# Order of the DMA issues in an attention stage: later loads, one-hot moves, the first head's operands and the gate's weights

## The chip, the core and the metric

The kernel runs on one core of a Trainium2 chip. The metric is the device time of one execution in microseconds (us). The kernel before took 1594.1 us, the median of three runs (1592.13 to 1594.23).

## What is computed

The reference chains three stages over 1536 tokens (2 batches of 768) with 512 features, all in float32:

- Attention with 8 heads of 64 features per batch, where a query sees only the keys of its own bucket. A bucket is the sign pattern of the vector's product with six random directions (`proj`). Scores are masked, go through a softmax, and weight `v`.
- A mixture of 8 experts (512 to 1024 to 512, ReLU), each applied to all tokens and weighted by a matrix `P`: the exponential of the gate's logits, balanced by 8 alternations of row and column normalization.
- A second mixture of 8 experts in which each token goes to one expert, assigned greedily by descending logit, 192 tokens to an expert.

```
mask = q_bucket[:, :, :, None] == k_bucket[:, :, None, :]
scores = np.where(mask, scale * q @ k.T, -1e9);  attn = softmax(scores);  x = attn @ v
P = balance(exp(x @ w_gate));  x = sum_e P[:, e] * (relu(x @ w1[e]) @ w2[e])
x[assigned == e] -> relu(x @ w1b[e]) @ w2b[e]
```

## The kernel before

The attention stage is a software pipeline written out by hand. The 16 heads are taken as 8 pairs (n = 0 to 7, two heads s = 0 and 1 of one batch), and each pair as 12 tiles of 128 query rows: tiles 0 to 5 of a pair belong to its first head, 6 to 11 to its second (`TU` = 12, r is the tile's number within its pair). Two tiles make a unit. `PLANS` lists, for even and for odd tiles, the steps and how many tiles each lags behind; the loop over t issues them in that order, and with `manual_schedule` every engine, SP included, executes its own instructions strictly in that order.

For a tile, TensorE forms the scores in PSUM from two products (`qk`, L277): `ka`,`qa` carry high and low parts of q and k, `kb`,`qb` another part and, in rows 64 to 127, one-hot rows of the buckets that do the masking. VectorE takes the maximum (L284), ACT the exponential (L289), POOL normalizes `e` (L301), TensorE transposes it (`tr`, L309), ACT and VectorE split it in high and low parts (L317, L321), and TensorE multiplies by V (`av`, L331). The result of a unit leaves through `xa`: for s = 0 ACT writes `xm` and SP moves its lower half to `xc` (L347); for s = 1 ACT writes `x1` (L351; a buffer called x, idle or pz) and SP moves it in two DMAs to `xm` and `xc` (L352, L353). Two tiles later POOL adds them and splits the sum into `X` (`xp`, L363 to L365). `xa` stands in even tiles, eight tiles behind its unit; so the second head's three units leave in r = 2, 4 and 6 of the next pair, and are added in r = 4, 6 and 8.

Beside a pair's tiles its successor is prepared (`prep`, one step in each of r = 0 to 9): r = 0 and 1 transpose q (from `rq`, L170) and split it, r = 2 and 3 do k, r = 4 and 5 compute bucket bits (L199), r = 6 to 9 the one-hots (`hot`, written by ACT, L230). The split operands and one-hots must get to other partitions, and SP's DMAs do that: `stack` collects such moves in `MOVES`, and at the end of a tile SP issues those that were there at its start (L159). So the six q moves come at the end of r = 2, the six k moves at the end of r = 4, two one-hot moves each at the ends of r = 8 and r = 10. Pair 0 is prepared ahead of the loop; its moves are issued at once for the first head, and held back (`HELD`) for the second.

`load(n)` brings a pair's q, k and v from HBM: two DMAs of 192 KB each to `rq`, `rk`, `rv`, which have two buffers each, so pair n + 2 takes the buffers of pair n, and its load waits for their last reader. Loads of pairs 0 and 1 are ahead of the loop; `load(n + 2)` stands in the last tile of pair n:

```
if r in (0, 2) and 0 < n < NP:
    prep_v(n, r // 2 + 2)
if r == TU - 1 and n + 2 < NP:
    load(n + 2)
```

`prep_v` are POOL's splits of `rv` into high and low parts of V (L254, L257). For n > 0 the last two of a pair stand in its tiles 0 and 2; for pair 0 all four stand in the loop's tiles 3, 3, 6 and 8 (`PREP_V`).

Behind the attention stage the first mixture begins: `wgr`, `wgs` are the gate's weights and their split (L465 to L469), `load_w1` and `load_w2` bring and split the first expert's weights (L431, L432, L436, L441), and `rows_to_cols` computes the logits (L480, L481).

Of the kernel before, what the change touches and what calls it, by code (L numbers as in the profile page):

```python
# [9 lines left out]
F32 = mybir.dt.float32  # L10
F32R = mybir.dt.float32r
# [3 lines left out]
AF = mybir.ActivationFunctionType  # L15
OP = mybir.AluOpType
# [22 lines left out]
def rd(x):  # L39
    return x.bitcast(F32)  # L40
# [3 lines left out]
def kernel(ctx, tc, q, k, v, proj, wg1, w1, w2, wg2, w1b, w2b, out):  # L44
    nc = tc.nc
    B, H, S, D = q.shape
    NB = proj.shape[1]
    N, Dm = out.shape
    E = wg1.shape[1]
    F = w1.shape[2]  # L50
    R = S // 128
    NP = B * H // 2
    HP = H // 2
# [4 lines left out]
    consts = ctx.enter_context(tc.tile_pool(name="consts", bufs=1))  # L58
# [10 lines left out]
    ap = actx.enter_context(tc.tile_pool(name="attn", bufs=1))  # L69
# [1 line left out]

    RAW = {}

    def load(n, what="qkv"):
        b, hp = divmod(n, HP)
        for nm, src in (("q", q), ("k", k), ("v", v)):
            if nm in what:
                t = ap.tile([128, R, 2, D], F32, name="r" + nm, bufs=2)
                rows = (slice(0, R // 2), slice(R // 2, R)) if n == 0 and nm != "v" else (slice(0, R),)
                for rs in rows:  # L80
                    for s in range(2):
                        nc.sync.dma_start(t[:, rs, s, :], src[b, 2 * hp + s].rearrange("(p r) d -> p r d", r=R)[:, rs])
                RAW["r" + nm, n] = t

    order = ExitStack()
    order.enter_context(tc.manual_schedule(engines=ENGINES))
    load(0, "qk")
    load(1, "q")
    idle = ap.tile([128, 512], BF, name="idle")
    nc.gpsimd.memset(idle, 0.0)  # L90
    nc.gpsimd.memset(ident, 1.0)
    nc.gpsimd.affine_select(ident, ident, pattern=[[-1, 128]], compare_op=OP.is_equal, fill=0.0,
                            base=0, channel_multiplier=1)
    pj0 = ap.tile([128, NB], F32, name="pj0")
    for s in range(2):
        nc.scalar.dma_start(pj0[64 * s:64 * s + 64], proj)
    nc.gpsimd.memset(zero, 0.0)
    pid = ap.tile([128, NB], I32, name="pid")
    nc.gpsimd.iota(pid, pattern=[[0, NB]], base=0, channel_multiplier=1)
    pj = ap.tile([128, 256], F32, name="pj")  # L100
    nc.gpsimd.memset(pj, 0.0)
    pz = ap.tile([128, 256], F32, name="pz")
    nc.gpsimd.memset(pz, 0.0)
# [15 lines left out]
    def warm(ns):  # L119

        for _ in range(round(ns / 214)):
            nc.tensor.matmul(Op.rearrange("p a b -> p (a b)"), idle[:, :128], idle, start=True, stop=True)

    warm(1500)
    pat = ap.tile([128, 2, 128], F32R, name="pat")
    pjh = ap.tile([128, 256], F32R, name="pjh")
    pjl = ap.tile([128, 256], F32R, name="pjl")
# [14 lines left out]

    HELD = []

    def stack(n, s, moves):

        if n == 0 and s == 1 and HELD is not None:
            HELD.append((n, s, moves))
            return
        MOVES.extend((dst[at:at + 64, s], src[64 * s:64 * s + 64]) for dst, at, src in moves)  # L150
        if n == 0:
            move()

    MOVES = []

    def move(n=None):

        for dst, src in MOVES[:n]:
            nc.sync.dma_start(rd(dst), rd(src))  # L159
        del MOVES[:n]  # L160

    def prep_t(n, nm, ch, part):
        x = RAW["r" + nm, n]
        c0, c1 = PC[ch]
        if part == 0:
            if ch == 0:
                PREP[nm, n] = [ap.tile([128, S], F32R, name=nm + x, bufs=2 if nm == "q" else 1) for x in ("hi", "lo")]
            t = aps.tile([128, 512], F32, name="tp", bufs=3)
            for r in range(c0 // 128, c1 // 128):
                nc.tensor.transpose(t[:, r * 128 - c0:r * 128 - c0 + 128],  # L170
                                    x[:, r].rearrange("p h d -> p (h d)"), ident)
            PREP["t"] = t[:, :c1 - c0]
            return
        hi, lo = PREP[nm, n]
        t = PREP["t"]
        if part == 1:
            nc.scalar.activation(hi[:, c0:c1], t, AF.Copy, scale=scale if nm == "q" else 1.0)
            return
        if nm == "q":
            nc.vector.scalar_tensor_tensor(lo[:, c0:c1], t, scale, rd(hi[:, c0:c1]), op0=OP.mult, op1=OP.subtract)  # L180
        else:
            nc.vector.tensor_tensor(lo[:, c0:c1], t, rd(hi[:, c0:c1]), op=OP.subtract)
        if ch == 0:
            return
        qa, ka, qb, kb = ST[n % 2]
        for s in range(2):
            stack(n, s, ((qa, 0, hi), (qa, 64, hi), (qb, 0, lo)) if nm == "q" else ((ka, 0, hi), (ka, 64, lo), (kb, 0, hi)))

    def prep_bits(n, ch, part):
        c0, c1 = PC[ch]  # L190
# [16 lines left out]
    def hot_rows(dst, t, w, s, on_dve=False):  # L207

        rows = slice(64 * s, 64 * s + 64)
        if on_dve:  # L210
            nc.vector.tensor_scalar(dst, t[rows], 0.5 * NB if w else 0.5 * (NB - 2), 1.0 if w else BIG,
                                    op0=OP.is_ge if w else OP.is_gt, op1=OP.subtract if w else OP.mult)
        else:
            nc.scalar.activation(dst, t[rows], AF.Sign if w else AF.Relu, bias=cb[rows, w:w + 1], scale=1.0 if w else BIG)

    def prep_hot(n, w, ch, part):
        c0, c1 = PC[ch]
        if part == 0:
            if ch == 0 and n:
                PREP["o", w, n] = ap.tile([128, S], F32R, name=f"hot{w}", bufs=1)  # L220
            t = (Sp[1] if n == 0 and w == ch == 1 else aps.tile([128, 512], F32, name="tp", bufs=3))[:, :c1 - c0]
            nc.tensor.matmul(t, pat[:, w], PREP["b", n][:, c0:c1], start=True, stop=True)
            PREP["t"] = t
        if part == 1 and n == 0:
            for s in range(2):
                hots0[s].append((ST[0][2 + w][64:128, s, c0:c1], PREP["t"], w, s))
            hot_rows(*hots0[0].pop(), on_dve=w != ch)
        elif part == 1:
            hot = PREP["o", w, n]
            nc.scalar.activation(hot[:, c0:c1], PREP["t"], AF.Sign if w else AF.Relu, bias=cb[:, w:w + 1],  # L230
                                 scale=1.0 if w else BIG)
            if ch == 1:
                dst = ST[n % 2][2 + w]
                for s in range(2):
                    stack(n, s, ((dst, 64, hot),))

    def prep(n, i, part):
        if i < 4:
            prep_t(n, "qk"[i // 2], i % 2, part)
        elif i < 6:  # L240
            prep_bits(n, i - 4, part)
        else:
            prep_hot(n, (i - 6) // 2, i % 2, part)
# [18 lines left out]
    TU = 4 * U  # L262
# [109 lines left out]
    def ahead_v(t):  # L372
        n, r = divmod(t, TU)
        for i in range(4):
            if t == PREP_V[i]:
                prep_v(0, i)
        if r in (8, 10) and n + 1 < NP:
            prep_v(n + 1, r // 2 - 4)
        if r in (0, 2) and 0 < n < NP:
            prep_v(n, r // 2 + 2)  # L380
        if r == TU - 1 and n + 2 < NP:
            load(n + 2)

    STEPS = dict(qk=qk, soft=soft, expo=expo, inv=inv, norm=norm, tr=tr, th=trh, tl=trl, av=av, xa=xa, xp=xp, pp=lambda t: ahead(t, 0), pa=lambda t: ahead(t, 1), pd=lambda t: ahead(t, 2),
# [28 lines left out]
    core = ctx.enter_context(tc.tile_pool(name="core", bufs=1, reuse_waits="tile"))  # L413
# [4 lines left out]
    def small_ps():  # L418
        return ps.tile([128, 512], F32, name="sp", bufs=2)
# [45 lines left out]
    wgr = core.tile([128, HP, E], F32, name="wgr")  # L465
    nc.sync.dma_start(wgr, wg1.rearrange("(a p) e -> p a e", p=128))
    wgs = core.tile([128, HP, 2 * E], F32R, name="wgs")
    nc.vector.tensor_copy(wgs[:, :, :E], wgr)
    nc.vector.tensor_tensor(wgs[:, :, E:], wgr, rd(wgs[:, :, :E]), op=OP.subtract)  # L469
# [27 lines left out]
    t = small_ps()  # L497
# [276 lines left out]
    for blk in range(NX):  # L774
        Hs.append((as_h(bigx() if blk else big()), as_h(big())))
        if blk == NX - 1:
# [5 lines left out]
            hot = hotp[:, :C * HC // 2].bitcast(F16).rearrange("p (c n) -> p c n", c=C)  # L782
# [434 lines left out]
```

## Time and profile before

| | us |
|---|---|
| Median of three runs | 1594.1 |
| The profiled execution, its own time | 1593.44 |
| Span of that execution, first to last instruction | 1591.7 |
| TensorE (PE) busy | 1548.0 |
| VectorE (DVE) busy | 809.2 |
| ACT busy | 453.2 |
| POOL busy | 269.9 |

The attention stage ends at about 270 us of the span; the first mixture fills the time to about 1279 us and the second the rest. A row of a timeline gives the start, the length, the engine and line, what is written from what, and how many instructions were merged; in brackets stands how long the engine stood idle before it and what it is thought to have waited for. SPq and ACTq are DMA issues on the queues of SP and ACT: their length is that of the issue, not of the transfer. L numbers are lines of the kernel before.

### The profile page before, as it was taken

To read this page: it belongs to the slowest core of one execution; us is meant where nothing else is said; L and a number is where in the kernel's file an instruction comes from. 1 tells how busy PE (TensorE), PEld (TensorE's weight loads), DVE (VectorE), ACT (ScalarE), POOL (GpSimd) and SP (SyncE) were. 2 spreads that over 40 slices of the span, in tenths; PEclk is the share of its full clock that TensorE was granted. 3 is DMA by queue.
4 is the path that set the end of the run, shared out by engine and by line. 5 is a ranking of instruction groups with operands and counts; after the bars stand their busy time and mean duration, and the time that the engine had idled before them with its cause. 6 is when DMAs were issued, how large, how long until landed. Compare 5 with 4: busy or idle time off the path is not lost.

```text
span 1591.7 us, 21428 instructions
## 1 busy us (share of the span) xinstructions
PE 1548.0 (97%) x8482; PEld 1311.2 (82%) x8482; DVE 809.2 (51%) x1833; ACT 453.2 (28%) x855; POOL 269.9 (17%) x313
## 2 busy tenths in 40 slices
PE   7999998999999999999999999999999999999998
PEld 6888886788888888888888888888887767788998
DVE  6888886712433334333333332134676377567533
ACT  6787886211211211221221021021121210011343
POOL 4888887020000000000000000000000000111221
PEclk9999999999999999999999999999999999899999
DMA  8766662220200110120020020011000116545531
GB/s 190 167 146 164 147 138 66 67 93 0 93 14 14 66 40 1 53 67 1 27 93 1 14 80 27 0 54 53 1 14 14 40 40 224 180 180 183 195 136 31
DMA packets 89301, 123.84 MB, mean 78 GB/s; under 512 B 44336, under 2 KB 52016, under 8 KB 89200
## 3 DMA queue, kind: packets, MB, share of 16 engines
q1 hardware_dynamic: 81680, 109.88, 23.7%
q0 software_dynamic: 2176, 6.29, 1.3%
q10 hardware_dynamic: 5344, 6.30, 1.1%
q8 instruction: 67, 1.10, 0.3%
q14 instruction: 34, 0.28, 0.1%
HBM read 83.91 MB, written 9.44 MB: 59 GB/s over the span
## 4 chain that ended last, share of the span: by engine, by line
PE 85%; DMA 4%; ACT 3%; DVE 2%; SPq 2%; POOL 2%; issue 1%; POOLq 0%; ACTq 0%; DVEq 0%
PE hp L567 32%; PE yp L586 29%; PE hp L944 5%; PE yp L888 4%; PE yp L997 3%; PE S L277 2%; PE O L331 2%; PE tp L309 2%; PE yp L1000 1%; PE sp L1081 1%; ACT e L289 1%; DMA rq<-in_q_dram 1%; SPq L159 1%; PE tp L199 1%; DMA raw<-in_moe_w_dram 1%
## 5 line engine op out<-in xcount | busy, mean ns | idle before, releaser
L567 PE MATMUL hp<-X,big 128*128 128x512 f32 x2304 | 528.9, 390 | 0.0
L567 PEld LDWEIGHTS hp<-X,big 128*128 128x128 f32 x2304 | 431.7, 188 | 89.9
L586 PE MATMUL yp<-big 128*128 128x512 f32 x2016 | 461.2, 389 | 0.0
L586 PEld LDWEIGHTS yp<-big 128*128 128x128 f32 x2016 | 378.2, 188 | 78.4
L568 ACT ACTIVATE big<-hp 128x512 fp32r<-128x512 f32 x176 | 105.2, 598 | 755.9 <-PE hp L567 755.9
L569 DVE SCALAR_TENSOR_TENSOR big<-hp,big 128x512 fp32r<-128x512 f32 x176 | 121.6, 691 | 252.3 <-ACT big L568 252.3
L591 DVE SCALAR_TENSOR_TENSOR acc<-yp,P,acc 128x512 f32<-128x512 f32 x72 | 54.1, 751 | 258.4 <-PE yp L586 258.4
L869 POOL DMA_INDIRECT raw<-x2h,who x4 | 4.1, 1025 | 949.5 <-DVE wg2b L1066 939.1
L301 POOL TENSOR_TENSOR e<-e,w 128x768 f32<-128x768 f32 x96 | 138.9, 1468 | 42.7 <-DVE w L296 27.5
L321 DVE TENSOR_TENSOR al<-tp,ah 128x512 fp32r<-128x512 f32 x144 | 98.2, 683 | 15.8 <-ACT ah L317 13.3
L284 DVE TENSOR_REDUCE w<-S 128x1 f32<-128x768 f32 x96 | 91.3, 951 | 14.8 <-PE S L277 13.4
L944 PE MATMUL hp<-raw,big 128*128 128x192 f32 x488 | 93.7, 338 | 1.2 <-ACT raw L922 1.2
L317 ACT ACTIVATE ah<-tp 128x512 fp32r<-128x512 f32 x144 | 86.2, 600 | 25.2 <-PE tp L309 22.2
L289 ACT ACTIVATE e<-S,w 128x768 f32<-128x768 f32 x96 | 87.0, 906 | 2.0 <-DVE w L284 1.9
L309 PE MATMUL tp<-ident,e 128*128 128x128 f32 x576 | 84.6, 274 | 2.2 <-POOL e L301 2.1
L432 DVE TENSOR_TENSOR big<-raw,big 128x1024 fp32r<-128x1024 f32 x63 | 76.6, 1222 | 14.1 <-ACT big L431 14.0
L944 PEld LDWEIGHTS hp<-raw,big 128*128 128x128 f32 x488 | 79.7, 193 | 2.8 <-ACT raw L922 1.7
L431 ACT ACTIVATE big<-raw 128x1024 fp32r<-128x1024 f32 x63 | 64.9, 1054 | 34.1 <-DMA raw<-in_moe_w_dram 32.8
L331 PE MATMUL O<-ah,vv 128*128 128x256 f32 x288 | 72.9, 283 | 1.3 <-ACT xm L346 0.8
L331 PE MATMUL O<-al,vv 128*128 128x256 f32 x288 | 72.9, 282 | 0.0
L309 PEld LDWEIGHTS tp<-ident,e 128*128 128x128 f32 x576 | 66.5, 141 | 4.8 <-POOL e L301 3.7
L542 DVE SCALAR_TENSOR_TENSOR junk<-acc,wg2b 128x512 bf16<-128x512 f32 x96 | 66.0, 687 | 1.9
(257 smaller groups left out, 1578.3 us busy)
## 6 DMA issues: line engine op xcount, KB each, us to landing
raw<-in_moe_w_dram SPq DMA_DIRECT2D x67, 512.0 KB, 3.4
big<-in_moe_w_dram SPq DMA_DIRECT2D x32, 1024.0 KB, 7.5
qa<-qhi SPq DMA_DIRECT2D x32, 192.0 KB, 3.8
qb<-qlo SPq DMA_DIRECT2D x16, 192.0 KB, 4.1
ka<-khi SPq DMA_DIRECT2D x16, 192.0 KB, 4.3
ka<-klo SPq DMA_DIRECT2D x16, 192.0 KB, 4.0
kb<-khi SPq DMA_DIRECT2D x16, 192.0 KB, 4.3
rv<-in_v_dram SPq DMA_DIRECT2D x16, 192.0 KB, 4.3
```

The lines of the kernel that those rows point to most:

```text
L284: nc.vector.tensor_reduce(EN[t][:, 0, i:i + 1], Sp[i], op=OP.max, axis=AX.X, negate=True)
L289: nc.scalar.activation(e, Sp[i], AF.Exp, bias=w[:, 0, i:i + 1], scale=1.0, accum_out=w[:, 1, i:i + 1])
L301: nc.gpsimd.tensor_tensor(e, e, w[:, 3, i:i + 1].to_broadcast([128, S]), op=OP.mult)
L309: nc.tensor.transpose(p[:, y * 128:y * 128 + 128], EN[t + i][:, kt * 128:kt * 128 + 128], ident)
L317: nc.scalar.activation(ah, TP[t, x], AF.Copy)
L321: nc.vector.tensor_tensor(al, TP[t, x], rd(ah), op=OP.subtract)
L331: nc.tensor.matmul(o, VS[n][:, kt, s].rearrange("p a d -> p (a d)"), a[:, :, kt], start=(kt == 0 and a is ah), stop=(kt == R - 1 and a is al))
L567: nc.tensor.matmul(t, a, b, start=(i == 0), stop=(i == len(prods) - 1))
L568: nc.scalar.activation(hh[:, f], t, AF.Relu)
L569: nc.vector.scalar_tensor_tensor(hl[:, f], t, 0.0, rd(hh[:, f]), op0=OP.max, op1=OP.subtract)
L586: nc.tensor.matmul(t, a, b, start=(i == 0), stop=(i == len(prods) - 1))
L944: nc.tensor.matmul(opened[f], w[:, d, f * 128:f * 128 + 128], xt[:, d], start=(d == 0), stop=(d == HP - 1))
```

## The change

- `load` gets a `queue` argument. At the start q of pair 0 is loaded on SP, then the projection (`pj0`) in one DMA and k of pair 0 on ACT's queue; six idle products warm TensorE and not seven.
- `pj` shares its buffer with an `x1` buffer.
- For the first head of pair 0 the operand rows are copied by engines: the three of q by POOL, two of k by ACT; only `klo` into `ka` goes by DMA.
- The one-hots of later pairs are moved at once, right behind ACT's writing of the second half, and not through `MOVES`.
- `load(n + 2)` stands in r = 3 and not in r = 11.
- The gate's weights are loaded ahead of the loop and split in tile 12, and not behind the attention stage.

```
--- before.py
+++ after.py
@@ -71,7 +71,7 @@
 
     RAW = {}
 
-    def load(n, what="qkv"):
+    def load(n, what="qkv", queue=None):
         b, hp = divmod(n, HP)
         for nm, src in (("q", q), ("k", k), ("v", v)):
             if nm in what:
@@ -79,25 +79,26 @@
                 rows = (slice(0, R // 2), slice(R // 2, R)) if n == 0 and nm != "v" else (slice(0, R),)
                 for rs in rows:
                     for s in range(2):
-                        nc.sync.dma_start(t[:, rs, s, :], src[b, 2 * hp + s].rearrange("(p r) d -> p r d", r=R)[:, rs])
+                        (queue or nc.sync).dma_start(t[:, rs, s, :],
+                                                     src[b, 2 * hp + s].rearrange("(p r) d -> p r d", r=R)[:, rs])
                 RAW["r" + nm, n] = t
 
     order = ExitStack()
     order.enter_context(tc.manual_schedule(engines=ENGINES))
-    load(0, "qk")
+    load(0, "q")
+    pj0 = ap.tile([128, NB], F32, name="pj0")
+    nc.scalar.dma_start(pj0, bass.AP(tensor=proj.tensor, offset=proj.offset, ap=[[0, 2], [NB, D], [1, NB]]))
+    load(0, "k", nc.scalar)
     load(1, "q")
     idle = ap.tile([128, 512], BF, name="idle")
     nc.gpsimd.memset(idle, 0.0)
     nc.gpsimd.memset(ident, 1.0)
     nc.gpsimd.affine_select(ident, ident, pattern=[[-1, 128]], compare_op=OP.is_equal, fill=0.0,
                             base=0, channel_multiplier=1)
-    pj0 = ap.tile([128, NB], F32, name="pj0")
-    for s in range(2):
-        nc.scalar.dma_start(pj0[64 * s:64 * s + 64], proj)
     nc.gpsimd.memset(zero, 0.0)
     pid = ap.tile([128, NB], I32, name="pid")
     nc.gpsimd.iota(pid, pattern=[[0, NB]], base=0, channel_multiplier=1)
-    pj = ap.tile([128, 256], F32, name="pj")
+    pj = ap.tile([128, 256], F32, name="x1")
     nc.gpsimd.memset(pj, 0.0)
     pz = ap.tile([128, 256], F32, name="pz")
     nc.gpsimd.memset(pz, 0.0)
@@ -121,7 +122,7 @@
         for _ in range(round(ns / 214)):
             nc.tensor.matmul(Op.rearrange("p a b -> p (a b)"), idle[:, :128], idle, start=True, stop=True)
 
-    warm(1500)
+    warm(1300)
     pat = ap.tile([128, 2, 128], F32R, name="pat")
     pjh = ap.tile([128, 256], F32R, name="pjh")
     pjl = ap.tile([128, 256], F32R, name="pjl")
@@ -142,14 +143,21 @@
 
     HELD = []
 
-    def stack(n, s, moves):
+    def stack(n, s, moves, nm=None):
 
         if n == 0 and s == 1 and HELD is not None:
             HELD.append((n, s, moves))
             return
-        MOVES.extend((dst[at:at + 64, s], src[64 * s:64 * s + 64]) for dst, at, src in moves)
-        if n == 0:
-            move()
+        for dst, at, src in moves:
+            to, x = dst[at:at + 64, s], src[64 * s:64 * s + 64]
+            if n:
+                MOVES.append((to, x))
+            elif s or (nm, at) == ("k", 64):
+                nc.sync.dma_start(rd(to), rd(x))
+            elif nm == "q":
+                nc.gpsimd.tensor_copy(to, rd(x))
+            else:
+                nc.scalar.activation(to, rd(x), AF.Copy)
 
     MOVES = []
 
@@ -184,7 +192,7 @@
             return
         qa, ka, qb, kb = ST[n % 2]
         for s in range(2):
-            stack(n, s, ((qa, 0, hi), (qa, 64, hi), (qb, 0, lo)) if nm == "q" else ((ka, 0, hi), (ka, 64, lo), (kb, 0, hi)))
+            stack(n, s, ((qa, 0, hi), (qa, 64, hi), (qb, 0, lo)) if nm == "q" else ((ka, 0, hi), (ka, 64, lo), (kb, 0, hi)), nm)
 
     def prep_bits(n, ch, part):
         c0, c1 = PC[ch]
@@ -232,7 +240,7 @@
             if ch == 1:
                 dst = ST[n % 2][2 + w]
                 for s in range(2):
-                    stack(n, s, ((dst, 64, hot),))
+                    nc.sync.dma_start(rd(dst[64:128, s]), rd(hot[64 * s:64 * s + 64]))
 
     def prep(n, i, part):
         if i < 4:
@@ -378,7 +386,7 @@
             prep_v(n + 1, r // 2 - 4)
         if r in (0, 2) and 0 < n < NP:
             prep_v(n, r // 2 + 2)
-        if r == TU - 1 and n + 2 < NP:
+        if r == 3 and n + 2 < NP:
             load(n + 2)
 
     STEPS = dict(qk=qk, soft=soft, expo=expo, inv=inv, norm=norm, tr=tr, th=trh, tl=trl, av=av, xa=xa, xp=xp, pp=lambda t: ahead(t, 0), pa=lambda t: ahead(t, 1), pd=lambda t: ahead(t, 2),
@@ -397,7 +405,13 @@
         stack(*x)
     load(0, "v")
     load(1, "v")
+    wgr = consts.tile([128, HP, E], F32, name="wgr")
+    nc.sync.dma_start(wgr, wg1.rearrange("(a p) e -> p a e", p=128))
+    wgs = consts.tile([128, HP, 2 * E], F32R, name="wgs")
     for t in range(NT + max(x[1] for x in PLANS[0])):
+        if t == TU:
+            nc.vector.tensor_copy(wgs[:, :, :E], wgr)
+            nc.vector.tensor_tensor(wgs[:, :, E:], wgr, rd(wgs[:, :, :E]), op=OP.subtract)
         due = len(MOVES)
         for nm, lag, *part in PLANS[t % 2]:
             if 0 <= t - lag < NT:
@@ -462,11 +476,6 @@
     ones = core.tile([128, 128], F32, name="ones")
     nc.gpsimd.memset(ones, 1.0)
 
-    wgr = core.tile([128, HP, E], F32, name="wgr")
-    nc.sync.dma_start(wgr, wg1.rearrange("(a p) e -> p a e", p=128))
-    wgs = core.tile([128, HP, 2 * E], F32R, name="wgs")
-    nc.vector.tensor_copy(wgs[:, :, :E], wgr)
-    nc.vector.tensor_tensor(wgs[:, :, E:], wgr, rd(wgs[:, :, :E]), op=OP.subtract)
     acc = core.tile([128, C, Dm], F32, name="acc")
 
     def rows_to_cols(stat, movs, dst):
```

## Rows read from the trace of the kernel before

**Rows 1.** The page: busy time of TensorE, and the exponential's group (busy us, mean ns).

```profile
PE 1548.0 (97%) x8482; PEld 1311.2 (82%) x8482; DVE 809.2 (51%) x1833; ACT 453.2 (28%) x855; POOL 269.9 (17%) x313
...
L289 ACT ACTIVATE e<-S,w 128x768 f32<-128x768 f32 x96 | 87.0, 906 | 2.0 <-DVE w L284 1.9
```

**Rows 2.** Busy time by stages: sum of six pair spans, 42.74 to 233.10 us.

```profile
sum 190.36, PE 178.02 PEld 167.20 DVE 163.85 ACT 155.85 POOL 160.84; mean PE 29.67 PEld 27.87 DVE 27.31 ACT 25.97 POOL 26.81
```

**Rows 3.** TensorE's waits, 0 to 275 us: us in total, times, longest.

```profile
PE S L277 <- DMA kb<-hot: 5.3, 6, 1.2
PE tp L170 <- DMA rq<-in_q_dram: 4.8, 4, 1.7
PE sp L480 <- DVE wgs L469: 4.3, 1, 4.3
...
PE tp L170 <- DVE w L296: 1.7, 2, 0.9
```

**Rows 4.** Timeline of SP's queue in pair 2: start, us of issue, line, transfer.

```profile
88.02 0.88 SPq L352 DMA_DIRECT2D xm<-idle  x1
88.95 0.85 SPq L353 DMA_DIRECT2D xc<-idle  x1
...
95.14 0.95 SPq L353 DMA_DIRECT2D xc<-pz  x1
...
104.11 1.34 SPq L82 DMA_DIRECT2D rq<-in_q_dram  x2
...
106.93 1.78 SPq L82 DMA_DIRECT2D rv<-in_v_dram  x2
```

**Rows 5.** Timeline of POOL in pair 2 (in brackets its wait, and for what).

```profile
88.00 2.89 POOL L301 TENSOR_TENSOR e<-e,w 128x768 f32<-128x768 f32 x2
91.72 0.74 POOL L363 TENSOR_TENSOR xm<-xm,xc 128x256 f32<-128x256 f32 x1 [0.82 <-DMA xc<-idle]
...
93.23 0.74 POOL L365 TENSOR_TENSOR X<-xm,X 128x256 fp32r<-128x256 f32 x1
...
98.01 0.73 POOL L363 TENSOR_TENSOR xm<-xm,xc 128x256 f32<-128x256 f32 x1
...
100.19 2.90 POOL L301 TENSOR_TENSOR e<-e,w 128x768 f32<-128x768 f32 x2
```

**Rows 6.** Timeline of TensorE in pair 2: transposes of `e`.

```profile
96.80 0.60 PE L309 MATMUL tp<-ident,e 128*128 128x128 f32 x4
...
101.72 0.66 PE L309 MATMUL tp<-ident,e 128*128 128x128 f32 x4
```

**Rows 7.** Line L82, all loads: time from issue to landing.

```profile
DMA to landing us min/median/max: 2.4/3.9/4.7
```

**Rows 8.** Timeline of SP's queue, the start and the end of pair 0.

```profile
2.92 2.08 SPq L82 DMA_DIRECT2D rk<-in_k_dram  x4
...
9.36 1.45 SPq L159 DMA_DIRECT2D ka<-klo  x1
...
17.56 0.91 SPq L159 DMA_DIRECT2D kb<-khi  x1
...
39.22 0.46 SPq L347 DMA_DIRECT2D xc<-xm  x1
39.72 1.24 SPq L159 DMA_DIRECT2D kb<-hot  x2
```

**Rows 9.** Timeline of TensorE: first score product of pair 0, second of pair 1.

```profile
13.65 0.62 PE L277 MATMUL S<-ka,qa 128*128 128x512 f32 x2 [2.15 <-DMA ka<-klo]
...
42.74 0.59 PE L277 MATMUL S<-kb,qb 128*128 128x512 f32 x2 [1.17 <-DMA kb<-hot]
```

**Rows 10.** Timeline of POOL: the last V copy of pair 0 (tile 8).

```profile
38.88 1.02 POOL L257 TENSOR_TENSOR vv<-rv,vv 128x384 fp32r<-128x384 f32 x1
```

**Rows 11.** By stages behind attention: us, busy by engine, granted clock, DMA share, GB/s.

```profile
269.50:273.80 4.30, 0.01 (x2) 0.01 (x1) 0.44 (x2) 0.38 (x1) 3.37 (x6) 1.00 0.45 94
274.00:278.00 4.00, 4.00 (x12) 1.36 (x11) 1.06 (x1) 1.83 (x2) 1.09 (x3) 0.57 0.92 334
```

More of the change, by code (lines that the diff above doesn't have):

```diff
@@ L72, with load @@
     RAW = {}
-    def load(n, what="qkv"):
+    def load(n, what="qkv", queue=None):
         b, hp = divmod(n, HP)
@@ L81, in load @@
                     for s in range(2):
-                        nc.sync.dma_start(t[:, rs, s, :], src[b, 2 * hp + s].rearrange("(p r) d -> p r d", r=R)[:, rs])
+                        (queue or nc.sync).dma_start(t[:, rs, s, :],
+                                                     src[b, 2 * hp + s].rearrange("(p r) d -> p r d", r=R)[:, rs])
                 RAW["r" + nm, n] = t
@@ L86 @@
     order.enter_context(tc.manual_schedule(engines=ENGINES))
-    load(0, "qk")
+    load(0, "q")
+    pj0 = ap.tile([128, NB], F32, name="pj0")
+    nc.scalar.dma_start(pj0, bass.AP(tensor=proj.tensor, offset=proj.offset, ap=[[0, 2], [NB, D], [1, NB]]))
+    load(0, "k", nc.scalar)
     load(1, "q")
@@ L93 @@
                             base=0, channel_multiplier=1)
-    pj0 = ap.tile([128, NB], F32, name="pj0")
-    for s in range(2):
-        nc.scalar.dma_start(pj0[64 * s:64 * s + 64], proj)
     nc.gpsimd.memset(zero, 0.0)
@@ L99 @@
     nc.gpsimd.iota(pid, pattern=[[0, NB]], base=0, channel_multiplier=1)
-    pj = ap.tile([128, 256], F32, name="pj")
+    pj = ap.tile([128, 256], F32, name="x1")
     nc.gpsimd.memset(pj, 0.0)
@@ L122, in warm @@
             nc.tensor.matmul(Op.rearrange("p a b -> p (a b)"), idle[:, :128], idle, start=True, stop=True)
-    warm(1500)
+    warm(1300)
     pat = ap.tile([128, 2, 128], F32R, name="pat")
@@ L143, with stack @@
     HELD = []
-    def stack(n, s, moves):
+    def stack(n, s, moves, nm=None):
         if n == 0 and s == 1 and HELD is not None:
@@ L149, in stack @@
             return
-        MOVES.extend((dst[at:at + 64, s], src[64 * s:64 * s + 64]) for dst, at, src in moves)
-        if n == 0:
-            move()
+        for dst, at, src in moves:
+            to, x = dst[at:at + 64, s], src[64 * s:64 * s + 64]
+            if n:
+                MOVES.append((to, x))
+            elif s or (nm, at) == ("k", 64):
+                nc.sync.dma_start(rd(to), rd(x))
+            elif nm == "q":
+                nc.gpsimd.tensor_copy(to, rd(x))
+            else:
+                nc.scalar.activation(to, rd(x), AF.Copy)
     MOVES = []
@@ L186, in prep_t @@
         for s in range(2):
-            stack(n, s, ((qa, 0, hi), (qa, 64, hi), (qb, 0, lo)) if nm == "q" else ((ka, 0, hi), (ka, 64, lo), (kb, 0, hi)))
+            stack(n, s, ((qa, 0, hi), (qa, 64, hi), (qb, 0, lo)) if nm == "q" else ((ka, 0, hi), (ka, 64, lo), (kb, 0, hi)), nm)
     def prep_bits(n, ch, part):
@@ L234, in prep_hot @@
                 for s in range(2):
-                    stack(n, s, ((dst, 64, hot),))
+                    nc.sync.dma_start(rd(dst[64:128, s]), rd(hot[64 * s:64 * s + 64]))
     def prep(n, i, part):
@@ L380, in ahead_v @@
             prep_v(n, r // 2 + 2)
-        if r == TU - 1 and n + 2 < NP:
+        if r == 3 and n + 2 < NP:
             load(n + 2)
@@ L399 @@
     load(1, "v")
+    wgr = consts.tile([128, HP, E], F32, name="wgr")
+    nc.sync.dma_start(wgr, wg1.rearrange("(a p) e -> p a e", p=128))
+    wgs = consts.tile([128, HP, 2 * E], F32R, name="wgs")
     for t in range(NT + max(x[1] for x in PLANS[0])):
+        if t == TU:
+            nc.vector.tensor_copy(wgs[:, :, :E], wgr)
+            nc.vector.tensor_tensor(wgs[:, :, E:], wgr, rd(wgs[:, :, :E]), op=OP.subtract)
         due = len(MOVES)
@@ L463 @@
     nc.gpsimd.memset(ones, 1.0)
[L465 to L469, printed above, removed]
     acc = core.tile([128, C, Dm], F32, name="acc")
```

## The prediction

> **What bounds the kernel now.** I read the page's busy times first: TensorE is busy for 1548.0 of 1591.7 us [rows 1], so only the stretches where it waits can give time back. The rest of the kernel behind the attention stage (two expert stages) is touched by the change only in its first microseconds, and I carry it over unchanged. The view by stages then shows the attention stage: six spans from one pair's start to the next take 190.36 us together, 31.73 each, with TensorE busy for 178.0 and POOL for 160.8 of them [rows 2]. TensorE idles 2.06 us a pair and POOL 4.9, so POOL is a second resource that is nearly full. Third, the list of TensorE's waits up to 275 us [rows 3] says where its idle time lies: 5.3 us on `kb<-hot` (six pair starts), 4.8 on `rq` (four pair starts), 1.7 more at the same place, the first transposes of `rq`, put down to a VectorE instruction long done, so I count it to `rq` too, and 4.3 us once on the gate's weights. Per pair start that is 0.88 for the one-hots and (4.8 + 1.7)/6 = 1.08 for `rq`, 1.96 together. The change attacks these.
>
> Last I read SP's own order within one pair, and POOL's and TensorE's beside it. This is where I expect the result to be decided. From its second tile on SP issues without a break: x moves, six q moves, x moves (88.02 and 88.95, the latter ending 89.80), six k moves, x moves (the last ends 96.09) [rows 4]. POOL needs each of these x moves two tiles later: it was free at 90.89 (88.00 + 2.89) and stood until 91.72 for `xc` (0.82 us); the next, at 98.01, came just in time [rows 5]. Behind the x additions POOL normalizes the next two tiles, from 100.19 on; the first is done at 101.64, and TensorE transposes it at 101.72 [rows 6]. So at this point the chain SP, POOL, TensorE has no slack at all.
>
> **The change part by part.**
>
> *Loads in the fourth tile.* They were issued in a pair's last tile, after the one-hots: 104.11 to 108.71, six issues, 4.6 us [rows 4]. They now stand in SP's order behind the six q moves and ahead of the x moves of tile 4. What they give: `rq` is there long before it is transposed, 1.08 us a pair start. What they cost: everything behind them on SP comes later by six issues. In the start of the program four such issues took 2.08 us, so six take 3.1 at least [rows 8]; 4.6 is the row of the same six; I take 4.4, nearest to the latter, because the transfers around them are as dense. Then `xc` of tile 4 lands at 96.1 and not at 91.72; POOL, free at 90.89, idles 5.2 us in place of 0.82. Its three additions (91.72 to 93.97, 2.25 us) and two normalizations (2.90) end at 101.25, one V copy (1.02 at most [rows 10]) by 102.3. The k moves and x moves behind the load end 4.4 later too: the last x move at 100.5, landing 1.92 later (89.80 to 91.72) at 102.4. So POOL's next x addition starts at 102.4 in place of 98.01, the normalization at 104.65 in place of 100.19, and TensorE's transpose moves from 101.72 to 106.1, 4.4 later; the one before it (96.80) moves by some 3.0. At the pair's end the two waits of 1.96 are gone. Net +2.4 us a pair. POOL works off its own delay in its other idle time, so the next pair starts from TensorE's delay alone and the amount repeats. It applies to pairs 1 to 5: pair 0 has no x additions, pairs 6 and 7 load nothing. 5 x 2.44 = **+12.2**. Bounds: 3.1 - 1.96 = 1.2 a pair (+5.8 in all); 4.6 and another 1.1 because the x moves' data may queue behind the load's (a load lands 3.9 after its issue [rows 7], the x move 91.72 - 88.95 = 2.8) less 1.96 = 3.7 a pair (+18.7).
>
> *The same load in pair 0.* `rv` has two buffers, and `rv` of pair 2 takes that of pair 0. Its last reader is the V copy that stands in tile 8, while the load now stands in tile 3. SP therefore stops at `rv` until POOL has done tile 8's copy (38.88 + 1.02 = 39.90 [rows 10]). Behind it on SP wait pair 1's k moves, all its one-hots and the x moves. With the faster start below (4.0 us) the release is at 35.9. Then two `rv` issues (1.8) to 37.7, six k moves (89.80 to 95.14 less one x issue of 0.9, 4.4) to 42.1, two one-hots of q (1.2) to 43.3, one x issue (0.5) to 43.8, and the first one-hot of k, which takes 3.0 from issue to use (39.72 to 42.74 [rows 8, 9]): 46.8 against 42.74, +4.1. Less the 0.9 of `rq` (half of 1.7 [rows 3]): +3.2. TensorE comes to this product at 42.74 - 1.17 - 4.0 = 37.6 [rows 9], so it has stood for 9.2 us. After 4.3 us of standing at 269.5 the granted clock was 0.57 for the next 4.0 us [rows 11], a loss of 1.7. Pair 1 so starts **+4.9** later than before (bounds +2.2, with a start faster by 5 and no loss of clock, to +6.4, with a start faster by 2.5).
>
> *The start itself.* Four `rk` issues go from SP (from 2.92) to ACT's queue behind one issue of `pj0`, so from about 1.4; bounded by nothing (if the transfers are what is slow) and 2.08, I take 1.3 on the last `k` residual. The `klo` move was issued at 9.36 behind three others and the first score product waited for it until 13.65, 4.3 us [rows 8, 9]; alone it should take 3.0, as the one-hot's did, so the product starts 2.5 earlier. Five moves less on SP and the transfers also bring the second head's `kb<-khi` (issued at 17.56, and waited for by pair 1's first k split) forward by about 5. Three POOL copies of 768 elements, about 1.45 each by the normalization's row (two of 768 elements in 2.90 [rows 5]), stand where POOL has nothing to do; two ACT copies at about 0.9 (the exponential's 768 elements, 906 ns [rows 1]) lie between the k splits and the one-hots, where ACT waited for TensorE. I take 4.0 for the start (2.5 to 5). All of it is contained in the +4.9 above: the release of SP hangs on it, and what was gained ahead of it is stood out at pair 1's start.
>
> *One-hots at once.* Now issued right after ACT wrote them, a tile and a half earlier, ahead of the x move that SP waited at. Six of the seven pair starts are settled above; the last gives **-0.9**. If SP stood at them for ACT, only an x move would be behind, needed four tiles later.
>
> *Gate's weights early.* TensorE's 4.3 us [rows 3] are mostly not on the path: the first expert's weights, split by ACT and VectorE, come later. What is on it is one SP issue ahead of these loads (0.6) and a shorter gate among VectorE's splits. I take **-1.2** (-0.6 to -2.5). The two small VectorE operations in tile 12 cost nothing while SP's moves hold TensorE there, 0.4 us at most otherwise. One idle warm-up product less lies beside `rq`'s arrival: 0.
>
> **Sum.** 12.2 + 4.9 - 0.9 - 1.2 = +15.0 against the profiled execution's 1593.4 us (span 1591.7; the median shown, 1594.1, is 0.04% above it): **1608 us**. The lowest sum of the bounds is 5.8 + 2.2 - 0.9 - 2.5 = +4.6 (1598), the highest 18.7 + 6.4 - 0.9 - 0.6 = +23.6 (1617).
>
> **The clock in each pair.** The row shows a clock of 0.57 after 4.3 us without work [rows 11]; a wait of 3 us in the middle of pairs 1 to 5 is not in this trace, and the sum above keeps 1.00 there. The Trainium skill ("TensorE: Matmul & The Clock Gate", HAM oscillation) has it that a wait that comes back in every pass of a loop can throw the array to its lower clock in every pass. By that rule the sum would be 1616.9, by the rows alone 1608.4; the trace agrees with it for the one long wait at 269.5 and shows nothing for shorter ones.
>
> **The rivals.**
> 1. *Faster: POOL absorbs the late x moves.* Place: the x addition of tile 6. If `xc` came no later than POOL is ready, by less than about 1.96 us net at TensorE, the pair starts' gain is kept. For it: POOL idles 4.9 us a pair. Against it: POOL already waits here, and 101.64 to 101.72 leaves 0.1. With none of the delay at TensorE: -9.8 in place of +12.2, 1586.4.
> 2. *SP isn't held in pair 0*, so pair 1 starts earlier by 4.0 + 1.17 + 0.9 = 6.1, and not later by 4.9: 1597.4; with rival 1 as well 1575.5. Against it: the reader of tile 8 is in the code.
> 3. *The clock falls in each pair:* 1.7 each, 8.5: 1616.9.
> 4. *The delay and the gain cancel* (a delay of 2 us a pair and a short hold in pair 0): about 1594.
>
> **How the numbers follow.** Forecast (1598 to 1617) 0.58; rival 3 0.08; rival 2 alone 0.10; rival 1, with or without 2, 0.17; rival 4 0.07. A difference under 0.2% (3.2 us) can't be told from none here. Slower: 0.58 + 0.08 and most of rival 2, 0.75; same: rival 4 and an edge, 0.07; faster: 0.18. The range that leaves out rival 1's half and the far end of rival 3 is 1589 to 1618.
>
> **What would show it.** In the new trace: SP's `rq`, `rk`, `rv` issues between q moves and x moves; POOL's wait for `xc<-idle` at some 5 us in pairs 1 to 5 (0.8 now); TensorE waiting for POOL's `e` by 3 to 4 us in the ninth tile; pair spans of about 34 us in place of 31.7; no wait for `rq`; SP standing 10 us before the third `rv`, and TensorE 8 us at pair 1's start. Wrong it would be if pair spans are under 31.5, or if pair 1 starts before 42.7.

## The result, and the profile after

The changed kernel takes **1612.52 us** (median of 4 runs, 1611.03 to 1618.63); the kernel before, on the same chip, 1593.12 (1591.51 to 1594.23). The ratio is 1.013, 95% interval 1.0102 to 1.0158: 19.4 us slower. The forecast was 1608 (1589 to 1618). The profiled execution of the changed kernel is its longest, 1618.63 us (span 1616.8), so its trace overstates the loss by about 6 us. In `prep`, `soft` and `tr` every line stands 8 further down than before (the normalization L301 is now L309, the transposes L309 are L317).

The page again begins with the busy times, beside [rows 1]:

```profile
PE 1562.4 (97%) x8481; PEld 1326.7 (82%) x8481; DVE 808.2 (50%) x1833; ACT 453.4 (28%) x857; POOL 271.8 (17%) x316
```

TensorE has one instruction less and 14.4 us more busy time. Most of that is work at a lower clock. The five passes from pair 1's first `rq` transpose to pair 6's show it by stages. The columns are the stretch and its us, then the busy time of each engine, granted clock, DMA share, GB/s. First the kernel before, then the changed one:

```profile
45.35:76.85 31.50, 29.65 (x221) 27.89 (x221) 27.14 (x49) 26.10 (x56) 26.95 (x25) 1.00 0.70 157
...
sum 158.97, PE 148.60 PEld 139.36 DVE 136.83 ACT 130.62 POOL 134.80; mean PE 29.72 PEld 27.87 DVE 27.37 ACT 26.12 POOL 26.96
```

```profile
49.92:87.23 37.31, 32.68 (x221) 31.16 (x221) 26.34 (x46) 25.51 (x55) 25.77 (x24) 0.86 0.57 133
...
sum 180.05, PE 158.54 PEld 150.35 DVE 134.09 ACT 129.51 POOL 133.65; mean PE 31.71 PEld 30.07 DVE 26.82 ACT 25.90 POOL 26.73
```

The passes went from 31.8 to 36.0 us each, 21.1 in all: 9.9 of it is longer TensorE work on the same instructions, 11.1 idle time. The first row's start also says that pair 1 begins 4.6 later. What is left of attention behind them, 0.6 shorter, and the gate, another 0.6 shorter, give little back.

Where TensorE waits, up to 295 us (us in total, times, longest), beside [rows 3]:

```profile
PE tp L317 <- POOL e L309: 23.3, 8, 4.6
PE S L285 <- DMA kb<-hot: 5.5, 1, 5.5
...
PE tp L178 <- DMA rq<-in_q_dram: 0.4, 1, 0.4
```

The waits that the change attacked are gone: `rq` has 0.4 us left, `kb<-hot` is left once, in pair 1, and the gate's weights are not in the list. In their place TensorE waits for POOL's normalized tiles, 23.3 us, once in each of pairs 1 to 5 by 4.0 to 4.6. POOL's own wait is this one:

```profile
POOL xm L371 <- DMA xc<-idle: 32.8, 5, 7.0
```

SP's queue in pair 2 says why, beside [rows 4]:

```profile
97.97 2.07 SPq L82 DMA_DIRECT2D rq<-in_q_dram  x2
100.09 1.34 SPq L82 DMA_DIRECT2D rk<-in_k_dram  x2
101.53 1.45 SPq L82 DMA_DIRECT2D rv<-in_v_dram  x2
103.08 0.84 SPq L360 DMA_DIRECT2D xm<-idle  x1
103.97 0.59 SPq L361 DMA_DIRECT2D xc<-idle  x1
```

The six loads hold SP from 97.97 to 102.98, 5.0 us, and the x moves stand behind them. POOL (beside [rows 5]) is free at 101.36, waits 6.2 us, and everything that it does after that is late. TensorE (beside [rows 6]) stands at 111.29:

```profile
98.47 2.89 POOL L309 TENSOR_TENSOR e<-e,w 128x768 f32<-128x768 f32 x2
107.59 0.73 POOL L371 TENSOR_TENSOR xm<-xm,xc 128x256 f32<-128x256 f32 x1 [6.23 <-DMA xc<-idle]
```

```profile
111.29 1.11 PE L317 MATMUL tp<-ident,e 128*128 128x128 f32 x4 [4.02 <-POOL e L309]
```

### The profile page after: what moved, and what is told of

Read it like the earlier page. It is cut to its first block, busy times and chain, and to the rows that moved or that the text cites. A ratio compares the mean times of both kernels' runs of the same rounds, so it can differ in the third digit from the quotient of the medians.

```text
span 1616.8 us, 21450 instructions
## 1 busy us (share of the span) xinstructions
PE 1562.4 (97%) x8481; PEld 1326.7 (82%) x8481; DVE 808.2 (50%) x1833; ACT 453.4 (28%) x857; POOL 271.8 (17%) x316
## 3 DMA queue, kind: packets, MB, share of 16 engines
q8 instruction: 66, 1.08, 0.3%
## 4 chain that ended last, share of the span: by engine, by line
PE 89%; DMA 3%; DVE 3%; POOL 2%; ACT 2%; issue 1%; SPq 0%; ACTq 0%; POOLq 0%; DVEq 0%
PE hp L576 32%; PE yp L595 28%; PE hp L953 5%; PE yp L897 4%; PE O L339 3%; PE tp L317 3%; PE S L285 3%; PE yp L1006 3%; PE yp L1009 1%; PE sp L1090 1%; DMA xc<-idle 1%; PE tp L207 1%; POOL e L309 1%; PE yp L1011 1%; PE tp L178 1%
## 5 line engine op out<-in xcount | busy, mean ns | idle before, releaser
L309 POOL TENSOR_TENSOR e<-e,w 128x768 f32<-128x768 f32 x96 | 138.9, 1468 | 35.3 <-DVE w L304 25.7
L317 PE MATMUL tp<-ident,e 128*128 128x128 f32 x576 | 89.5, 285 | 23.3 <-POOL e L309 23.3
L317 PEld LDWEIGHTS tp<-ident,e 128*128 128x128 f32 x576 | 70.3, 147 | 26.0 <-POOL e L309 24.9
L339 PE MATMUL O<-ah,vv 128*128 128x256 f32 x288 | 76.4, 293 | 1.4 <-ACT xm L354 0.9
L445 ACT ACTIVATE big<-raw 128x1024 fp32r<-128x1024 f32 x63 | 64.7, 1053 | 33.8 <-DMA raw<-in_moe_w_dram 32.5
```

Of the source, the lines that this page charges most:

```text
L309: nc.gpsimd.tensor_tensor(e, e, w[:, 3, i:i + 1].to_broadcast([128, S]), op=OP.mult)
L317: nc.tensor.transpose(p[:, y * 128:y * 128 + 128], EN[t + i][:, kt * 128:kt * 128 + 128], ident)
L339: nc.tensor.matmul(o, VS[n][:, kt, s].rearrange("p a d -> p (a d)"), a[:, :, kt], start=(kt == 0 and a is ah), stop=(kt == R - 1 and a is al))
```

## The experiments

Each edit is to the changed kernel unless it says otherwise; `r` is the tile within a pair, `TU` its 12 tiles. Each ratio is to the kernel before on the same chip. The runs stand on several chips, on which the kernel before took 1593.1 to 1594.5 us, so some differences are given by the ratios too.

**Load back in the last tile** (the rest of the change stays):

```diff
-        if r == 3 and n + 2 < NP:
+        if r == TU - 1 and n + 2 < NP:
```

> The changed kernel with the loads of later pairs back in a pair's last tile; all else of the change stays. Theory A (the load's place in SP's queue is what costs: x moves behind it reach POOL late in pairs 1 to 5, and SP is held in pair 0): POOL's wait for xc falls from 6 to 7 us a pair to under 1, pair spans from about 35.4 to 30 to 30.7 us, pair 1 starts near 37 us, and the time is 1576 to 1584 us, clearly under the kernel before. Theory B (the cost lies in another part: engine copies, one-hots at once, or the early gate): the time stays above 1600 us and pair spans above 33.

1578.76 us (1574.64 to 1580.11), ratio 0.9909 (0.9889 to 0.993). So the move of the loads costs 33.8 us (1612.52 - 1578.76), and all else in the change gains 14.4. The waits of TensorE, of POOL, and the five passes:

```profile
PE tp L178 <- DMA rq<-in_q_dram: 2.5, 4, 0.9
...
PE tp L178 <- DVE w L304: 1.5, 1, 1.5
```

```profile
POOL xm L371 <- DMA xc<-idle: 2.4, 5, 0.8
```

```profile
sum 152.07, PE 147.23 PEld 139.22 DVE 139.46 ACT 130.22 POOL 134.27; mean PE 147.23 PEld 139.22 DVE 139.46 ACT 130.22 POOL 134.27
```

POOL's wait is back at under 1 us a pair, and the passes are 30.4 us, against 31.8 before the change. The expectation of 1576 to 1584 us held. At the first transposes of `rq` TensorE still waits: 4.7 us in six pair starts by the timeline, against 6.5 before. So there an earlier load had up to 4.7 us left to give.

**The two halves of the move.** Only pair 0's load back in the last tile, and its opposite, only pair 0's load in the fourth:

```diff
+        if r == (3 if n else TU - 1) and n + 2 < NP:     # first kernel
+        if r == (TU - 1 if n else 3) and n + 2 < NP:     # second kernel
```

> The changed kernel with pair 0's load alone back in its last tile; pairs 1 to 5 load in their fourth. Theory A: SP is not held before the third rv, pair 1 starts 8 to 9 us earlier than the 47.0 of the changed kernel and without the slow clock behind it, 1600 to 1604 us; pair spans of pairs 1 to 5 stay at 35 to 36. Rival (the hold in pair 0 only takes up time that would be lost anyway): under 3 us gained, 1609 to 1613.

> The changed kernel with the early load in pair 0 alone; pairs 1 to 5 load in their last tile. Theory A: the hold stays (pair 1 starts near 47), pair spans fall from 35.4 to 30 to 30.7: 1585 to 1592 us. Rival (pair 0's hold is most of the loss): above 1600. If the two places add up, this run's gain and that of the run with pair 0 last sum to the gain of the run with all loads last.

The first takes 1605.62 us (1603.06 to 1607.28; ratio 1.0076, 1.0059 to 1.0093): without pair 0's hold 6.9 are back, and the kernel is still slower than before (1600 to 1604 was expected). The second takes 1584.21 (1582.34 to 1589.01; ratio 0.9943, 0.9926 to 0.9959): the hold alone costs 5.4 against the loads in the last tile (1585 to 1592 was expected). The effects add up within 1.4 us: undoing the move in pair 0 gains 6.9, undoing it in the other pairs 28.3 (1612.52 - 1584.21), 35.2 together, against 33.8 in one. POOL's wait in the first and TensorE's in the second:

```profile
POOL xm L371 <- DMA xc<-idle: 33.7, 5, 7.1
```

```profile
PE S L285 <- DMA kb<-hot: 5.6, 1, 5.6
```

**The load's move alone, and the one-hots alone**, each put into the kernel before:

```diff
-        if r == TU - 1 and n + 2 < NP:      # first kernel
+        if r == 3 and n + 2 < NP:
-                    stack(n, s, ((dst, 64, hot),))      # second kernel
+                    nc.sync.dma_start(rd(dst[64:128, s]), rd(hot[64 * s:64 * s + 64]))
```

> The kernel before with one part of the change alone, the loads in the fourth tile. Theory A: without the faster start SP is released at 39.9 us, pair 1 starts near 51 us, pair spans go to 35 to 36: 1616 to 1628 us, slower than the changed kernel. Rival (the load's place is harmless by itself and the loss comes with another part): 1580 to 1593 us, as the waits for rq go.

> The kernel before with the one-hots moved at once, nothing else. Theory: 0.88 us at each of seven pair starts go, and the loads, now issued 1.2 us earlier behind one move less, give part of the 1.08 for q: 1581 to 1588 us. Rival (the next wait at the pair start takes its place): 1591 to 1594 us.

The loads alone: 1626.73 us (1625.65 to 1627.27), ratio 1.0212 (1.0195 to 1.0229). That is 33.5 over the 1593.21 beside it, the same price as in the changed kernel (33.8). TensorE's waits show both faults at once, POOL's late tiles and the one-hots in the list of moves: one wait of 6.1 at pair 1's start, behind pair 0's hold, and five of about 1.1, as before the change:

```profile
PE tp L309 <- POOL e L301: 25.2, 7, 5.8
...
PE S L277 <- DMA kb<-hot: 11.4, 6, 6.1
```

The one-hots alone: 1584.56 us (1583.4 to 1588.39), ratio 0.9941 (0.9921 to 0.9962), 9.9 us faster than the 1594.47 beside it. Its five passes:

```profile
sum 151.90, PE 147.41 PEld 139.35 DVE 137.09 ACT 129.47 POOL 133.71; mean PE 147.41 PEld 139.35 DVE 137.09 ACT 129.47 POOL 133.71
```

That is the same 30.4 a pass as with the rest of the change and late loads. One line, with the loads where they were, brings TensorE's idle time in the passes from 10.4 us (158.97 - 148.60) to 4.5. Nearly all of what is left stands at the first transposes of `rq`, 4.5 us in six pair starts by the timeline (6.5 before): that is what an earlier load could still have given.

**Does the clock cost?** Behind each of these five waits the granted clock is at or near 0.50 for some 4 to 6 us; that is the lower of its two levels (1.2 of 2.4 GHz). In the next kernel TensorE transposes the identity while it would stand, in pairs 1 to 5:

```diff
+        if x == 0 and t % TU == 4 and 1 <= t // TU <= 5:
+            for _ in range(32):
+                nc.tensor.transpose(p[:, :128], ident, ident)
```

> The changed kernel with 32 idle transposes on TensorE ahead of the first transposes of tile 8 in pairs 1 to 5, where it stands 4.0 to 4.6 us waiting for POOL (about 3.5 us of work that nobody reads). Theory: the lower clock behind that wait costs 1.7 us a pair; with TensorE kept at work the granted clock stays at 1.00 there, POOL's waits stay as they are, pair spans fall from 36.0 by 1.5 to 2, and the time is 1602 to 1606 us. Rival (POOL sets the pace, the clock costs nothing): 1611 to 1614, or more by the work added.

1611.85 us (1611.51 to 1613.53), ratio 1.0104 (1.0086 to 1.0122): 0.7 less than 1612.52, or 4 by the ratios (1.013 and 1.0104), whose intervals overlap, so the two are not told apart. The five passes take 177.35 us, 2.7 less than the 180.05 of the changed kernel; the expectation was 1.5 to 2 for each. A stretch with the clock, in the changed kernel (TensorE stood for 4.63 us until 76.08) and with the filling (columns as above); then TensorE's and POOL's rows with the filling:

```profile
74.00:80.00 6.00, 3.92 (x16) 3.73 (x17) 1.65 (x2) 1.95 (x4) 5.84 (x7) 0.50 0.55 139
```

```profile
74.00:80.00 6.00, 4.52 (x35) 4.14 (x34) 2.46 (x4) 3.57 (x7) 5.84 (x8) 1.00 0.50 129
```

```profile
75.66 0.66 PE L320 MATMUL tp<-ident,e 128*128 128x128 f32 x4 [1.48 <-POOL e L309]
81.50 0.66 PE L320 MATMUL tp<-ident,e 128*128 128x128 f32 x4 [1.11 <-POOL e L309]
```

```profile
71.96 0.73 POOL L374 TENSOR_TENSOR xm<-xm,xc 128x256 f32<-128x256 f32 x1 [7.29 <-DMA xc<-idle]
```

The clock is at its higher level, and TensorE then waits for POOL at the next tile. POOL is busy for 5.84 of the 6 us in both: it sets the pace here, and most of the time of the slow matmuls lay beside it.

**Issues or bytes?** For pairs 2 to 7 the six loads stay in their places, but each brings 8 KB into a scratch tile, and the pair is computed from the data of pairs 0 and 1 (so the output is another; pair 0's hold is gone too, so it compares with 1605.62):

```diff
+                if n > 1:
+                    RAW["r" + nm, n] = RAW["r" + nm, n % 2]
+                    few = ap.tile([128, 2, 16], F32, name="few" + nm)
+                    for s in range(2):
+                        nc.sync.dma_start(few[:, s], src[b, 2 * hp + s]....[:, 0, :16])
+                    continue
```

> The changed kernel with the six DMA issues in the fourth tile kept, but each moves 8 KB in place of 192 KB into a tile that nobody reads; pairs 2 to 7 are computed from the data of pairs 0 and 1, and nothing holds SP in pair 0. Theory 1 (it is SP's issue time that delays the x moves): POOL's wait for xc stays at about 4 us in pairs 1 to 5, and the time is 1590 to 1596 us. Theory 2 (it is the bytes ahead of them): POOL's wait is under 1.2 us as before the change, and the time is 1570 to 1576 us. Between the two: the share of each.

1594.89 us (1590.97 to 1596.67), ratio 0.9998 (0.9988 to 1.0008). Against 1578.76 the issues alone cost 16.1 us, and the bytes 10.7 more (1605.62 - 1594.89); by the ratios it is 14 and 12. This kernel has no `rq` waits at the pair starts either, so the issues' price is larger if anything. SP's queue and POOL:

```profile
86.30 1.91 SPq L82 DMA_DIRECT2D fewq<-in_q_dram  x2
88.26 0.91 SPq L82 DMA_DIRECT2D fewk<-in_k_dram  x2
89.21 0.90 SPq L82 DMA_DIRECT2D fewv<-in_v_dram  x2
90.21 0.47 SPq L366 DMA_DIRECT2D xm<-idle  x1
90.72 0.59 SPq L367 DMA_DIRECT2D xc<-idle  x1
```

```profile
92.79 0.73 POOL L377 TENSOR_TENSOR xm<-xm,xc 128x256 f32<-128x256 f32 x1 [3.07 <-DMA xc<-idle]
```

Six issues of next to nothing hold SP for 3.8 us, and the x move lands 1.5 after its issue has ended (91.31 to 92.79); behind full loads it is 5.0 and 3.0 (104.56 to 107.59). Over pairs 1 to 5 it is 3.4 to 4.5 and 1.5 to 2.2 here, 5.0 to 5.9 and 2.5 to 3.8 in the changed kernel.

**Other places for the loads**: in the sixth tile (pair 0's in the eleventh), and in the eleventh for all, right behind the last urgent one-hots:

```diff
+        if r == (5 if n else 10) and n + 2 < NP:     # first kernel
+        if r == 10 and n + 2 < NP:                   # second kernel
```

> The changed kernel with the loads in r = 5 (pairs 1 to 5; pair 0 in r = 10, so that SP is not held there): in SP's queue they stand behind the k moves and ahead of the x moves of r = 6. Theory (the place in SP's queue ahead of x moves): POOL's wait for xc<-idle falls to about 1 us, and in its place it waits 5 to 7 us for xc<-pz in each of pairs 1 to 5; 1598 to 1606 us, near the run with pair 0 last (1605.6). Rival (only the stretch with q and k moves together is too full): 1575 to 1582 us.

> The changed kernel with the loads in tile 10 of a pair, right behind the one-hots of k and ahead of an x move that is needed many tiles later. Theory: SP is free there, the x moves of tiles 2 to 6 are not behind it, and q lands before it is transposed: TensorE's 2.5 + 1.5 us of waits at that place in the run with the loads last go, 1573 to 1577 us. Rival: the last tile is early enough, no difference to 1578.8 beyond 1 us.

The first takes 1616.71 us (1611.63 to 1617.85; ratio 1.0148, 1.0131 to 1.0165). The wait moved to the next x move as expected, but its price was missed by 10.7 us at least: TensorE's waits for POOL are 33.3 us, against 23.3 in the changed kernel. Why less of the delay is absorbed here was not tried. POOL's and TensorE's waits:

```profile
POOL xm L371 <- DMA xc<-pz: 31.4, 5, 6.8
POOL xm L371 <- DMA xc<-idle: 1.9, 4, 0.8
```

```profile
PE tp L317 <- POOL e L309: 33.3, 7, 6.8
```

The second takes **1577.04 us** (1573.91 to 1579.26; ratio 0.9886, 0.9868 to 0.9904). It beats both kernels; from the 1578.76 of the twelfth tile it is not told apart, so neither expectation is settled.

**x moves past the loads.** Loads in the fourth tile, but not pair 0's; both x moves of the second head issued by ACT:

```diff
-            nc.sync.dma_start(xm[D:], x1[:D])
-            nc.sync.dma_start(xc[D:], x1[D:])
+            nc.scalar.dma_start(xm[D:], x1[:D])
+            nc.scalar.dma_start(xc[D:], x1[D:])
+        if r == (3 if n else 10) and n + 2 < NP:
```

> The changed kernel with loads in the fourth tile (pair 0's in r = 10), where the two x moves of a second head's unit are issued by ACT on its own queue, right behind the x tile that it writes. Theory 1 (SP's order and its ring are the whole delay): POOL's wait for xc<-idle is under 1.5 us, pair spans 30 to 31.5; six issues on ACT of 0.5 to 0.9 us each a pair cost up to 5 us of an engine busy 26 of 31.7: 1577 to 1592 us against 1605.6 with these moves on SP. Theory 2 (the load's bytes on the shared 16 DMA engines are the delay): POOL still waits 2 to 4 us, 1595 us or more.

1592.14 us (1589.2 to 1596.47; ratio 0.9996, 0.9985 to 1.0007), 13.5 less than 1605.62 with the x moves on SP (13 by the ratios). That is at the edge of theory 1's range, and 13.4 are still missing to the 1578.76 with late loads. ACT issues the moves beside SP's loads (the row of `rq` holds a gap, each of its two issues takes 0.59), and TensorE's waits for POOL are nearly gone. SP's queue, ACT's queue, POOL, TensorE's waits:

```profile
83.58 3.80 SPq L82 DMA_DIRECT2D rq<-in_q_dram  x2
```

```profile
86.52 0.47 ACTq L360 DMA_DIRECT2D xm<-idle  x1
87.03 0.61 ACTq L361 DMA_DIRECT2D xc<-idle  x1
```

```profile
86.92 0.74 POOL L371 TENSOR_TENSOR xm<-xm,xc 128x256 f32<-128x256 f32 x1 [2.42 <-DMA xc<-x]
...
91.97 0.73 POOL L371 TENSOR_TENSOR xm<-xm,xc 128x256 f32<-128x256 f32 x1
```

```profile
PE tp L178 <- DVE al L329: 6.2, 6, 1.7
PE tp L230 <- ACT hot L238: 4.1, 6, 1.4
...
PE tp L317 <- POOL e L309: 1.0, 2, 0.6
```

POOL does not wait for the moves that stood behind the loads (no bracket at 91.97). But it waits for those of the unit before, `xc<-x`, which ACT issues beside SP's q moves, once in each of pairs 2 to 6 and 8.0 us in all: the one shown was issued by 81.95, and POOL could start at 86.92. In pairs 1 to 6 the `xc` moves took 4.5 us from issue to landing on ACT's queue (median, 2.0 to 5.8), against 2.4 (2.0 to 3.6) on SP's queue with late loads. Pair 6, which loads nothing, has one of 4.4 too: that does not need a load beside it. So leaving SP's order is worth 13.5 us, half of what the move costs in pairs 1 to 5; that the order is the whole loss is not shown. The Trainium skill ("DMA: Bandwidth & Descriptors", Issuing engines are not separate DMA queues) says that issuing on several engines saves only the time of the sequencer, usually small against the DMA itself; here leaving SP's order is worth 13.5 us. A pass is still 32.2 us, not 30.4 (30 to 31.5 was expected): TensorE now waits for VectorE's and ACT's operands (the first two rows of its waits). Whether that comes from the issues on ACT, and what else the other 13.4 us are, was not tried.

## Why the prediction was right, and where its steps missed

**The cause and the sign were right.** SP's order, POOL without slack, TensorE one tile behind: each link is in the trace after, and the loads' move alone turns a gain of 14.4 into a loss of 19.4. From the runs the loss is -14.4 (loads late), +26.9 (the move in pairs 1 to 5, 1605.62 - 1578.76, counted from passes that the rest of the change had already shortened) and +6.9 (pair 0's hold): +19.4. The forecast set the shortening of the pair starts, 1.96 us a pair, against the move's delay, 4.4, within one term. The shortening was sized about right: with late loads the passes are 1.4 shorter, and 0.8 a pair start is left of the `rq` waits. The delay was too small: against late loads the passes of the changed kernel are longer by 5.1 (filled) to 5.6 us.

**Pairs 1 to 5, +12.2 predicted (bounds 5.8 to 18.7).** The passes lengthened by 3.7 (filled kernel: 177.35 / 5 = 35.5) to 4.2 us, 18.4 to 21.1 in all, at the upper bound or past it. Two prices were short: the six issues take 5.0 to 5.9 and not 4.4, and the x move lands 2.5 to 3.8 after its issue and not 1.92; a later landing was put into the upper bound alone. POOL's wait so came to 6.2 to 7.0 in place of 5.2, TensorE's to 4.0 to 4.6 in place of 3 to 4.

**Pair 0's hold, +4.9.** Pair 1's product was to start at 46.8 and did at 47.01. That is luck: three errors cancel. The last reader of `rv` was misread: the V copy of tile 8 is not the row in [rows 10], which belongs to the next pair, but this one of the kernel before, done 4.6 us earlier (35.28 and not 39.90):

```profile
34.26 1.02 POOL L257 TENSOR_TENSOR vv<-rv,vv 128x384 fp32r<-128x384 f32 x1
```

In the changed kernel it is done at 34.70 (POOL), SP issues `rv` at 34.73 after a wait of 4.8 us and not 10, and TensorE stood for 5.5 and not 8 to 9. POOL, SP's queue and TensorE there:

```profile
33.68 1.02 POOL L265 TENSOR_TENSOR vv<-rv,vv 128x384 fp32r<-128x384 f32 x1
```

```profile
34.73 1.23 SPq L82 DMA_DIRECT2D rv<-in_v_dram  x2
...
43.26 1.23 SPq L243 DMA_DIRECT2D kb<-hot  x2
```

```profile
47.01 0.98 PE L285 MATMUL S<-kb,qb 128*128 128x512 f32 x2 [5.54 <-DMA kb<-hot]
```

The faster start was oversized by 3.4: 4.0 us were taken, and the V copy came 0.6 earlier. The third error is the chain from SP's release to the product, 12.3 us and not 10.9, most of it in the issue and landing of the one-hots. At the start the first score product came 1.2 earlier (12.44, against 13.65 in [rows 9]), and TensorE waited for `rk` until 7.98, though ACT had issued it. The kernel before, then the changed one:

```profile
7.61 0.52 PE L170 MATMUL tp<-ident,rk 128*128 128x128 f32 x3 [0.89 <-DMA rk<-in_k_dram]
```

```profile
7.98 0.52 PE L178 MATMUL tp<-ident,rk 128*128 128x128 f32 x3 [1.42 <-DMA rk<-in_k_dram]
...
12.44 0.59 PE L285 MATMUL S<-ka,qa 128*128 128x512 f32 x2 [0.57 <-DMA ka<-klo]
```

The second issuing engine did not bring `rk` sooner here, with SP issuing `rq` of pairs 0 and 1 meanwhile. By the runs the hold costs 5.4 to 6.9; the forecast's 4.9 together with the 6.1 that it set for no hold is 11.

**One-hots, -0.9 beside 0.88 a pair start.** The term was right as far as it went, 6.2 over seven starts; alone on the chip it is 9.9. A part of the rest is in the `rq` waits, of which 4.5 us are left then, not 6.5; the remainder was not taken apart. So the forecast of what the earlier load gives, 1.08 a pair start or 6.5 over six, credited it with some 2 us that other parts of the same change take away.

**Gate, -1.2.** From the last attention product to the experts' steady block the changed kernel is 0.6 shorter (61.4 to 60.8), with late loads 3.0 (58.4); within the bounds at one end, just past them at the other.

**The rivals.** 1 (POOL absorbs) falls by the first half kernel, which has no hold and is 12.4 slower than before. 2 (SP not held) falls by SP's wait of 4.8 us and pair 1's late start. 4 falls by the result. 3 is half right: the clock does fall in each of these pairs. The Trainium skill ("TensorE: Matmul & The Clock Gate", HAM oscillation) says that a wait in every pass can do that; the trace agrees with it. The price of rival 3, 8.5 us, was not there: with the clock at its higher level the time is lower by 0.7 us, or 4 by the ratios, since POOL ends last in these stretches either way.

**What is left open:** why two `rq` issues take 2.07 us behind q moves and 1.3 elsewhere, and what in the changed kernel's longest execution took 6 us more than in the others.

## What to carry to other kernels

In a queue that works in order, price a moved load by what then stands behind it: look in the queue's own timeline for a stretch without gaps, and for the consumer with no slack; its place is right behind the last urgent move. Before two parts of a change are credited with the same wait, take each out alone: here one line held most of the gain and the other part all of the loss. Name the last reader of a buffer by its tile, not by its line, and count a drop of the clock only if TensorE ends last in that stretch.

## What was not expected of the hardware

- A DMA's issue has a price of its own: six of 8 KB took 3.4 to 4.5 us on SP, six full loads 5.0 to 5.9 in the same place; in pair 2 the first two, right behind the q moves, took 1.91 and 2.07.
- A small move behind full loads in one queue landed 2.5 to 3.8 us after its issue had ended, behind small ones 1.5 to 2.2.
- The `xc` moves issued on ACT's queue, beside SP's own moves and loads, took 4.5 us from issue to landing (median), against 2.4 on SP's queue with late loads.
- The clock stood at or near 0.50 for 4 to 6 us in a pair, and giving it back was worth 0.7 to 4 us of 1612.5, which is within the runs' spread.
